# Loading over two queues, softmax inside its PSUM banks, gates and attention weights moved by DMA, and a new order in a one-core transformer block

## The chip, the cores and the metric

The kernel runs on one core of a Trainium2 chip. A core has five instruction streams that work in parallel and meet at semaphores: TensorE (PE in the profile; its weight loads are PEld), VectorE (DVE), ScalarE (ACT), GpSimd (POOL) and SyncE (SP, which here only issues transfers). Transfers are issued by SP or ACT and carried by 16 DMA engines between HBM and the on-chip SBUF. Matmuls write to PSUM, eight banks of 2 KB per partition.

The metric is the device time of one execution in microseconds. The kernel before takes 247.15 us, the median of three runs from 247.07 to 247.26.

## The reference

One sequence of 2048 rows of 512 elements goes through an attention half and a feed-forward half. Both are modulated by a vector `c`.

```python
mod = (silu(c) @ w_mod).reshape(1, 6, 1, -1)
sa, ca, ga, sb, cb, gb = (mod[:, i] for i in range(6))
h = layernorm(x) * (1 + ca) + sa
x = x + ga * A(h, A_wqkv, A_wo)
h = layernorm(x) * (1 + cb) + sb
x = x + gb * B(h, B_w_gate, B_w_up, B_w_down)
```

A is attention with 32 heads of 16 elements. Each row s looks at 8 rows only: s, s-2, ... s-14. `logits = q . k / 4`, with rows before the start masked, a softmax over the 8, and the weighted sum of v, then `@ wo`. B is `(gelu(x @ w_gate) * (x @ w_up)) @ w_down` with 1792 hidden elements. Operands are bf16.

## The kernel before

The 2048 rows are cut into four blocks of 512 rows (`sg` in the code, "block" here), and a block into four chunks of 128 rows (`c4`). Each block goes through the same stages:

- **First norm** (`ln1`): BATCH_NORM_STATS and its aggregate on DVE per chunk (`st`, `mv`), the power -1/2 on POOL (`rstd`), and `xn` on DVE. Block 3's sums are made on ACT instead (`norm_act`).
- **Transpose and modulation** (`transp`, `transp_ev`): `xn` is turned so that features lie on partitions. It is done by PE, 16 matmuls of 128x128 against an identity, for the events in `BY_PE`, and by one DMA transpose on SP for all others; block 0's first norm has its own `transp0`. Then four ACT operations apply scale and shift (`hT` for attention, `h` for the FFN; h0 to h3 in the text).
- **qkv**: twelve groups of four 128x512 matmuls, each moved out of PSUM by an ACT cast into `qT`, `kT` or `vT`.
- **V by DMA** (`vload`): `vT` is stored to DRAM (`vscr`), and four loads bring shifted copies back as `V`, so that the neighbours of a row lie side by side. There is one `V` buffer.
- **Logits**: `pq`, q times eight shifted k, four DVE products of 128x4096 per block; strips of 32 output rows on PE sum them per head into `LTp` (`logits_mm`), which takes two PSUM banks.
- **Softmax** (`soft`): mask for block 0, maximum `mx`, subtraction `z`, exp on ACT, sum `ssum`, reciprocal `rinv`, product `e` (the operation is called p in the text).
- **Turning the weights**: 16 strip matmuls on PE (`PTp`), and two ACT casts into `PT`.
- **Weighted v**: four DVE products `pv` of 128x4096, strips on PE (`o_ps`), ACT casts `oT`, four x_ps groups with `wo`, and `x<-x_ps,x` on DVE, the residual.
- **Second norm** as the first, into `xn2`, then **FFN**: 14 pairs of `g_ps` and `u_ps` groups, gelu (`gl`) and cast (`ub`) on ACT, `hht` = gl x ub on DVE (hh in the text), then `y_ps`, 14 matmuls per chunk, `ot` on DVE and a store per chunk.

Modulation: four of the six parts of `mod` are columns (16 matmuls with one moving column, `cols`, L283); the gates `ga` and `gb` are wanted as rows on all partitions (`gB`), so `row` (L299) multiplies with a broadcast of silu(c), `scB`, in four 128x512 matmuls and an ACT cast. `woscale` and `wdscale` multiply `wo` and `w_down` by the gates on DVE.

**What sets the order.** Each stage is a generator of `Op`s (engine, planned duration, function, events it comes after, buffer slots it takes and gives). `ORDER` at the top of the file, a list of generator numbers, says which generator gives the next operation. The order is thus fixed by hand or by a planner beforehand, and the durations in the `Op`s have no effect on the chip. Each engine executes its own operations strictly in this order, so an instruction that waits holds everything behind it on its engine. This is true of SP's queue of transfers as well: an entry that waits for a semaphore holds the entries behind it.

Slots: `NB` gives buffers per pool, in PSUM `mm` 4 banks, `att` 2, `lg` 2 (one `LTp`). `prod` holds `pq` and `pv`, three buffers.

The head: SP issues x of block 0, chunks 0 and 1, then the `w_mod` parts 1 and 0 (`wm`), then the first third of `wqkv`, x of block 1, and so on (`sp_q`, L259). ACT's queue issues chunk 2, `c` and chunk 3 (`act_q`, L254). PE runs matmuls on zeros (`warmup`) until the first real ones.

In the order of SP's queue before, V of block 0 follows its store directly, then come vT of block 1, `Wg` and `Wu`.

Of the kernel before, what the change touches and what calls it, by code (L numbers as in the profile page):

```python
# [15 lines left out]
NEG = -4.0e9  # L16

ORDER = [
    2, 1, 4, 4, 4, 2, 4, 4, 4, 0, 4, 4, 4, 4, 4, 4, 4, 0, 4, 1, 1, 12, 12, 2, 12, 12, 12, 2, 2, 12, 12, 12, 12,
    12, 3, 3, 12, 12, 4, 4, 4, 4, 3, 3, 13, 3, 3, 3, 11, 13, 14, 2, 2, 2, 2, 2, 2, 2, 4, 4, 14, 14, 4, 4, 2, 11,  # L20
    11, 2, 2, 2, 11, 0, 4, 11, 33, 33, 33, 5, 33, 15, 15, 33, 15, 16, 15, 15, 16, 16, 16, 15, 15, 15, 16, 16,
    16, 18, 75, 15, 15, 15, 16, 15, 33, 75, 75, 33, 33, 33, 33, 16, 16, 16, 16, 34, 34, 75, 75, 35, 6, 2, 2, 2,
    35, 35, 54, 35, 18, 2, 2, 2, 7, 19, 19, 7, 18, 18, 19, 19, 36, 36, 75, 36, 75, 37, 20, 20, 20, 54, 37, 54,
    54, 6, 54, 54, 36, 36, 36, 20, 37, 37, 20, 20, 75, 7, 20, 7, 75, 75, 36, 36, 75, 54, 54, 54, 54, 37, 37, 37,
    20, 20, 20, 10, 36, 75, 75, 75, 75, 55, 55, 38, 2, 2, 37, 56, 56, 56, 56, 36, 36, 36, 37, 37, 21, 21, 37,
    21, 76, 76, 57, 57, 57, 77, 77, 22, 58, 58, 58, 57, 57, 57, 58, 77, 77, 23, 57, 22, 22, 58, 58, 58, 21, 23,
    57, 57, 22, 57, 39, 39, 23, 23, 37, 24, 24, 59, 25, 25, 26, 26, 57, 24, 25, 58, 58, 58, 58, 24, 25, 78, 40,
    78, 26, 26, 26, 78, 79, 2, 79, 79, 39, 39, 26, 78, 78, 78, 78, 26, 26, 26, 26, 79, 79, 79, 79, 78, 40, 27,
    27, 79, 57, 28, 78, 78, 78, 28, 28, 28, 79, 79, 79, 8, 38, 38, 38, 58, 38, 41, 41, 41, 78, 79, 29, 60, 60,
    8, 29, 29, 29, 30, 30, 30, 41, 61, 41, 30, 41, 41, 41, 41, 29, 31, 2, 2, 2, 9, 2, 29, 29, 29, 42, 42, 30,  # L30
    30, 30, 30, 29, 29, 29, 43, 31, 31, 30, 31, 30, 30, 42, 42, 29, 44, 29, 44, 29, 29, 30, 30, 31, 31, 29, 29,
    43, 30, 30, 30, 44, 59, 59, 29, 9, 9, 9, 30, 30, 44, 31, 9, 9, 9, 29, 60, 29, 29, 29, 31, 31, 30, 30, 30,
    45, 45, 46, 29, 59, 30, 29, 47, 46, 29, 47, 30, 30, 45, 45, 31, 31, 46, 46, 29, 29, 29, 31, 30, 30, 30, 30,
    47, 47, 47, 31, 31, 29, 29, 29, 47, 47, 47, 47, 47, 60, 29, 31, 31, 61, 48, 49, 59, 49, 29, 29, 29, 62, 49,
    49, 62, 81, 62, 50, 32, 32, 31, 50, 81, 29, 50, 51, 51, 62, 50, 51, 50, 51, 51, 62, 62, 52, 52, 31, 50, 50,
    51, 51, 62, 62, 62, 52, 82, 32, 50, 63, 63, 51, 50, 50, 51, 51, 50, 50, 51, 50, 51, 52, 52, 52, 64, 50, 63,
    80, 51, 51, 50, 50, 51, 51, 50, 50, 65, 51, 65, 50, 63, 64, 51, 50, 50, 50, 52, 52, 52, 65, 65, 81, 81, 80,
    80, 80, 66, 66, 67, 67, 51, 51, 50, 50, 68, 68, 51, 66, 52, 66, 67, 67, 82, 68, 51, 51, 50, 52, 51, 50, 50,
    50, 51, 68, 68, 68, 32, 83, 51, 51, 51, 50, 52, 52, 52, 50, 50, 50, 50, 50, 68, 68, 80, 68, 83, 83, 68, 69,
    52, 52, 70, 70, 50, 50, 53, 83, 83, 83, 83, 70, 70, 52, 83, 83, 71, 71, 71, 53, 52, 72, 72, 72, 71, 71, 72,  # L40
    71, 71, 71, 53, 84, 84, 73, 72, 72, 72, 72, 85, 71, 71, 71, 73, 73, 72, 86, 86, 71, 72, 72, 71, 71, 73, 71,
    72, 84, 84, 85, 72, 72, 71, 71, 71, 86, 86, 73, 73, 73, 87, 87, 72, 72, 72, 72, 71, 71, 73, 71, 71, 72, 71,
    72, 73, 72, 73, 72, 72, 88, 88, 87, 87, 88, 73, 71, 88, 71, 72, 71, 71, 71, 89, 89, 89, 72, 89, 89, 89, 72,
    72, 72, 73, 71, 73, 73, 89, 89, 89, 89, 71, 71, 71, 71, 71, 90, 91, 91, 91, 91, 53, 73, 73, 71, 71, 92, 74,
    92, 93, 93, 73, 74, 92, 73, 92, 92, 74, 74, 92, 93, 93, 93, 94, 94, 93, 92, 92, 93, 92, 93, 93, 94, 92, 92,
    92, 92, 93, 93, 93, 92, 92, 92, 94, 93, 93, 92, 94, 92, 93, 93, 94, 94, 94, 93, 93, 92, 93, 92, 92, 94, 92,
    93, 94, 93, 93, 92, 92, 92, 94, 93, 93, 93, 92, 92, 92, 93, 93, 93, 92, 94, 94, 94, 92, 92, 92, 92, 92, 94,
    94, 92, 92, 95, 95, 94, 95, 94, 94, 95, 95,
# [52 lines left out]
def kernel(  # L101
# [13 lines left out]
    nc = tc.nc  # L115
# [12 lines left out]
    def pool(name, bufs, **kw):  # L128
# [4 lines left out]
    NB = {"x": 4, "hT": 2, "xn": 2, "q": 4, "vs": 1, "v4": 1, "prod": 3, "lt": 1, "ot4": 1, "h2": 2,  # L133
          "wm": 1, "hh": 16, "o": 2, "wA": 3, "mm": 4, "att": 2, "lg": 1}
    pools = {k: pool(k + "_p", NB[k]) for k in NB if k not in ("mm", "att", "lg", "wm")}
    for k in ("mm", "att", "lg"):
        pools[k] = pool(k + "_p", NB[k], space=PSUM)
    pools["wm"] = pool("wm_p", NB["wm"])
    SL = {k: Slots(NB.get(k, 1)) for k in list(NB) + ["es", "PT"]}
    dram = pool("dram", 1, space=bass.MemoryType.DRAM)  # L140
    vscr = dram.tile([P, 4, VR], BF16, name="vscr")

# [15 lines left out]
    scB = const.tile([P, 4, P], BF16, name="scB")  # L158
# [49 lines left out]
    WM = {1: "h2", 0: "h2", 2: "wm", 3: "h2", 4: "h2", 5: "wm"}  # L208

    def loads():  # L210
# [13 lines left out]
        def ldwm(b, q=nc.sync):  # L224
            def f():
                B["wm", b] = T(WM[b], [P, 4, D], BF16, "wm")
                q.dma_start(
                    out=B["wm", b][:], in_=w_mod[:, b * D:(b + 1) * D].rearrange("(t p) n -> p t n", p=P))
            return f
# [4 lines left out]
        def mb(n):  # L234
            return n / 0.332
# [18 lines left out]
        def act_q():  # L254
            yield Op("ACT", 0.46, ldx(0, 2, 3, nc.scalar), fire="x0.2", lat=0.3, dma=True)
            yield Op("ACT", 0.46, ldc, fire="c", lat=0.0, dma=True)
            yield Op("ACT", 0.46, ldx(0, 3, 4, nc.scalar), fire="x0.3", lat=2.0, dma=True)

        def sp_q():  # L259
            for k in (0, 1):  # L260
                yield Op("SP", 0.47, ldx(0, k, k + 1), fire=f"x0.{k}", lat=0.3)
            yield Op("SP", 0.47, ldwm(1), take=[SL[WM[1]]], fire="wm1", lat=1.0)
            yield Op("SP", 0.5, ldwm(0), take=[SL[WM[0]]], fire="wm0", lat=1.85)
# [6 lines left out]
            yield Op("SP", 0.55, ldwm(2), take=[SL[WM[2]]], fire="wm2", lat=mb(0.5))  # L270
            yield Op("SP", 0.6, ldwm(3), take=[SL[WM[3]]], fire="wm3", lat=mb(0.5))
            yield Op("SP", 0.6, ldwm(4), take=[SL[WM[4]]], fire="wm4", lat=mb(0.5))
            for i in range(4):
                yield Op("SP", 0.45, ld(woP[H * i:H * i + H, :, :], wo_v[i]), fire=f"wo{i}", lat=0.5)
            yield from vload(0)
            yield Op("SP", 0.65, ld(Wg[:], wg_v), fire="Wg", lat=mb(1.75))
            yield Op("SP", 0.65, ld(Wu[:], wu_v), fire="Wu", lat=mb(1.75))
            yield Op("SP", 0.6, ldwm(5), take=[SL[WM[5]]], fire="wm5", lat=mb(0.5))
# [20 lines left out]
    def row(b, dst):  # L299
        def f():  # L300
            ps = T("mm", [P, D], F32, "mb_ps")
            for kt in range(4):
                nc.tensor.matmul(ps[:], lhsT=scB[:, kt, :], rhs=B["wm", b][:, kt, :], start=(kt == 0),
                                 stop=(kt == 3))
            B["mb", b] = ps

        def g():
            nc.scalar.copy(out=dst[:], in_=B["mb", b][:])
        return f, g
# [20 lines left out]
    def mods_ga():  # L330
        f, g = row(2, gB)
        yield Op("PE", 0.9, f, after=["wm2", "scB"], take=[SL["mm"]], give=[SL["wm"]], fire="mb2")
        yield Op("ACT", 0.58, g, after=["mb2"], give=[SL["mm"]], fire="ga")
# [6 lines left out]
    def mods_gb():  # L340
        f, g = row(5, gB)
        yield Op("PE", 0.9, f, after=["wm5", "scB", "woS"], take=[SL["mm"]], give=[SL["wm"]], fire="mb5")
        yield Op("ACT", 0.58, g, after=["mb5"], give=[SL["mm"]], fire="gb")

    def wdscale():
        for h in range(7):
            def wds(h=h):
                w = B["Wd", h // 2][:, 2 * (h % 2):2 * (h % 2) + 2, :]
                nc.vector.tensor_tensor(out=w, in0=w, in1=_ap(gB[:], [[0, 2], [1, D]]), op=ALU.mult)
            yield Op("DVE", 0.63, wds, after=["gb", f"Wd{h // 2}"], fire=f"WdS{h}")  # L350

    def woscale():
        def wos():
            nc.vector.tensor_tensor(out=woP[:], in0=woP[:], in1=_ap(gB[:], [[0, 4], [1, D]]), op=ALU.mult)
        yield Op("DVE", 1.15, wos, after=["ga"] + [f"wo{i}" for i in range(4)], fire="woS")

    def mods2():
        def f1():
            nc.scalar.copy(out=scB[:], in_=_ap(scT[:], [[1, 4], [0, P]]))
        yield Op("ACT", 0.65, f1, after=["scT", "LN1.0.h3.1"], fire="scB")  # L360
# [3 lines left out]
    def norm_act(key, src, ready, ev):  # L364
        k = {}

        for c4 in range(CPS):
# [6 lines left out]
            yield Op("ACT", 0.85, f, after=ready(c4), take=[SL["gl"]], give=[SL["gl"]], fire=f"{ev}.sa{c4}")  # L374
# [3 lines left out]
        yield Op("ACT", 0.2, f, fire=f"{ev}.nm")  # L378

        for c4 in range(CPS):  # L380
# [3 lines left out]
            yield Op("ACT", 0.85, f, take=[SL["gl"]], give=[SL["gl"]], fire=f"{ev}.sq{c4}")  # L384
# [511 lines left out]
```

## Time and profile before

| | us |
|---|---|
| median of three runs | 247.15 |
| the profiled execution | 247.37 |
| its span, first to last instruction | 245.5 |
| first qkv matmul starts | 10.84 |
| first pv of block 0 starts | 41.12 |
| last xn of block 0's second norm ends | 67.25 |
| first FFN matmul starts | 73.83 |
| last `ot` starts | 242.45 |

Times inside the execution count from the start of the span; a timeline row gives start, length and the instruction. The granted clock of TensorE was 1.000 over the span. On PE, a group of four 128x512 matmuls follows the next every 0.86 us. On DVE, the starts of successive instructions of one kind lie closer than the lengths of their rows, because the rows overlap: `pq` and `pv` follow each other every 2.21 us (row 2.28), st with mv every 0.80, an xn every 0.325, the residual every 0.62.

A row of a wait list has who waits, for whom, how long in total, how often, and the longest. A row of a group has line, engine, operation, output and inputs with shapes, count, then busy time and mean ns, then the engine's idle time ahead of it.

### The profile page before, as it was taken

What the parts mean: (1) busy time and instruction counts of PE and PEld (TensorE: products, weight loads), DVE (VectorE), ACT (ScalarE), POOL (GpSimd) and SP (SyncE); (2) the same over time, 40 slices, a digit from 0 to 9 for tenths busy, and PEclk for the clock granted to TensorE, in tenths of its full rate; (3) what the DMA queues carried; (4) which work ended last, traced back from release to release, by engine and by line L of the source; (5) the groups of instructions that cost most, each with busy time, mean ns of one, the idle gap of its engine ahead of it and who ended that gap; (6) DMA issues with size and microseconds to landing.
All of it is one profiled execution on the core that took longest, in us unless ns stands there. A gap on an engine that the chain in (4) does not pass through costs nothing.

```text
span 245.5 us, 3731 instructions
## 1 busy us (share of the span) xinstructions
PE 235.3 (96%) x1431; PEld 110.9 (45%) x1445; DVE 180.0 (73%) x253; ACT 144.0 (59%) x252; POOL 16.6 (7%) x37
## 2 busy tenths in 40 slices
PE   7899678999999999999999999999999999999994
PEld 2655345544453444444444444444444444444444
DVE  4789899989999899898989898677824922222222
ACT  2379698883688576325765835268654424666400
POOL 3450011000400000010000001000000100000000
PEclk9999999999999999999999999999999999999999
DMA  6998699959916009209300592400000061000011
GB/s 168 379 382 269 124 201 250 415 189 217 202 46 208 0 7 211 45 16 201 108 1 3 105 223 44 128 23 0 3 0 0 0 131 64 1 0 3 0 43 43
DMA packets 29289, 27.32 MB, mean 111 GB/s; under 512 B 7256, under 2 KB 28120, under 8 KB 29272
## 3 DMA queue, kind: packets, MB, share of 16 engines
q1 hardware_dynamic: 28976, 26.83, 42.3%
q10 hardware_dynamic: 296, 0.26, 0.4%
q8 instruction: 11, 0.18, 0.3%
q14 instruction: 6, 0.05, 0.1%
HBM read 21.32 MB, written 4.19 MB: 104 GB/s over the span
## 4 chain that ended last, share of the span: by engine, by line
PE 79%; DVE 13%; DMA 4%; POOL 1%; issue 1%; POOLq 0%
PE u_ps L763 19%; PE g_ps L763 19%; PE y_ps L775 18%; PE qkv_ps L556 8%; PE x_ps L735 6%; DMA x<-in_A_x_dram 4%; DVE pq L611 4%; PE o_ps L714 3%; PE LTp L625 2%; DVE st L419 2%; DVE ssum L658 1%; POOL rstd L429 1%; PE y_ps L786 1%; DVE e L669 1%; DVE mx L642 1%; DVE z L648 1%
## 5 line engine op out<-in xcount | busy, mean ns | idle before, releaser
L763 PE MATMUL u_ps<-h,Wu 128*128 128x512 bf16 x224 | 57.5, 379 | 0.0
L763 PE MATMUL g_ps<-h,Wg 128*128 128x512 bf16 x224 | 57.5, 379 | 0.0
L796 ACT ACTIVATE gl<-g_ps 128x512 bf16<-128x512 f32 x56 | 33.6, 601 | 24.9 <-PE g_ps L763 20.6
L775 PE MATMUL y_ps<-Wd,hht 128*128 128x512 bf16 x203 | 45.9, 379 | 0.4
L803 ACT CAST ub<-u_ps 128x512 bf16<-128x512 f32 x56 | 33.0, 589 | 18.2 <-PE u_ps L763 18.1
L814 DVE TENSOR_TENSOR hht<-gl,ub 128x512 bf16<-128x512 bf16 x56 | 22.3, 419 | 29.1 <-ACT ub L803 29.0
L556 PE MATMUL qkv_ps<-hT,wqkv 128*128 128x512 bf16 x184 | 42.2, 380 | 0.0
L700 DVE TENSOR_TENSOR pv<-PT,V 128x4096 bf16<-128x4096 bf16 x16 | 35.8, 2286 | 2.1 <-ACT PT L689 2.1
L611 DVE TENSOR_TENSOR pq<-qT,kT 128x4096 bf16<-128x4096 bf16 x16 | 36.0, 2283 | 0.9 <-PE o_ps L714 0.7
L763 PEld LDWEIGHTS <-Wu 128*128 128x128 bf16 x224 | 21.4, 98 | 27.6 <-issue 2.5
L763 PEld LDWEIGHTS <-Wg 128*128 128x128 bf16 x224 | 21.6, 98 | 26.8 <-issue 1.3
L775 PEld LDWEIGHTS <-hht 128*128 128x128 bf16 x210 | 20.5, 98 | 25.0 <-issue 0.4
L556 PEld LDWEIGHTS <-wqkv 128*128 128x128 bf16 x184 | 20.2, 114 | 19.0 <-issue 2.3
L429 POOL TENSOR_TENSOR rstd<-rstd,neghalf 128x4 f32<-128x4 f32 (+1 forms) x8 | 11.7, 1462 | 174.0 <-DVE rstd L425 174.0
L821 DVE TENSOR_TENSOR ot<-y_ps,x 128x512 bf16<-128x512 f32 x15 | 10.3, 688 | 17.1 <-PE y_ps L775 13.6
L419 DVE BATCH_NORM_STATS2 st<-x 128x6 f32<-128x512 bf16 x28 | 18.9, 675 | 3.0 <-DMA x<-in_A_x_dram 2.9
L489 ACT ACTIVATE h<-h,modT,scl 128x512 bf16<-128x512 bf16 x12 | 8.8, 802 | 15.9 <-DMA h<-xn 15.9
L735 PE MATMUL x_ps<-woP,oT 128*128 128x512 bf16 x60 | 14.9, 379 | 0.2
L570 ACT CAST qT<-qkv_ps 128x512 bf16<-128x512 f32 x16 | 9.5, 601 | 6.5 <-PE qkv_ps L556 5.6
L744 DVE TENSOR_TENSOR x<-x_ps,x 128x512 bf16<-128x512 f32 x16 | 10.7, 684 | 2.7 <-PE x_ps L735 2.7
L572 ACT CAST kT<-qkv_ps 128x512 bf16<-128x512 f32 x16 | 9.5, 602 | 2.8 <-PE qkv_ps L556 2.8
L436 DVE TENSOR_SCALAR xn<-x,mv,rstd 128x512 bf16<-128x512 bf16 x28 | 9.8, 407 | 1.6 <-POOL rstd L429 1.6
(76 smaller groups left out, 175.8 us busy)
## 6 DMA issues: line engine op xcount, KB each, us to landing
V<-vscr SPq DMA_DIRECT2D x12, 520.0 KB, 9.2
wm<-in_w_mod_dram SPq DMA_DIRECT2D x6, 512.0 KB, 7.5
vscr<-vT SPq DMA_DIRECT2D x4, 512.0 KB, 3.8
out_dram<-ot SPq DMA_DIRECT2D x15, 128.0 KB, 1.7
Wg<-in_B_w_gate_dram SPq DMA_DIRECT2D x1, 1792.0 KB
Wu<-in_B_w_up_dram SPq DMA_DIRECT2D x1, 1792.0 KB, 12.8
wqkv<-in_A_wqkv_dram SPq DMA_DIRECT2D x3, 512.0 KB, 8.1
x<-in_A_x_dram SPq DMA_DIRECT2D x3, 512.0 KB, 8.0
```

The costliest lines, as they stand in the source:

```text
L419: nc.vector.bn_stats(out=st_k["st"][:, c4, :], in_=src()[:, c4, :])
L429: nc.gpsimd.tensor_tensor(out=st_k["rstd"][:, a:b], in0=st_k["rstd"][:, a:b], in1=neghalf[:, a:b], op=ALU.pow)
L556: nc.tensor.matmul(ps[:], lhsT=wqkv[blk][:, dt, j::4], rhs=B["hT", sg][:, :, dt, :], start=(dt == 0), stop=(dt == DT - 1))
L611: nc.vector.tensor_tensor(out=pq[:], in0=_ap(B["qT", sg][:, j, :], [[0, W], [1, SG]]), in1=_ap(kT[:, j, sg * SG + 2:sg * SG + 2 + SG], [[2 ...
L700: nc.vector.tensor_tensor(out=t[:], in0=_ap(B["PT", sg][:, 0, :], [[SG, 2], [0, 4], [1, SG]]), in1=_ap(v[:, 0, j, :], [[8, 2], [4 * (SG + ...
L735: nc.tensor.matmul(ps[:], lhsT=B["oT", sg][:, j, c4 * P:(c4 + 1) * P], rhs=woP[:, j, :], start=(j == 0), stop=(j == 3))
L744: nc.vector.tensor_tensor(out=x[:, c4, :], in0=B["x1ps", sg, c4][:], in1=x[:, c4, :], op=ALU.add)
L763: nc.tensor.matmul(ps[:], lhsT=Wt[:, dt, ft * P:(ft + 1) * P], rhs=B["h2T", sg][:, :, dt, :], start=(dt == 0), stop=(dt == DT - 1))
L775: nc.tensor.matmul(ps[:], lhsT=B["hh", sg, ft][:, c4 * P:(c4 + 1) * P], rhs=B["Wd", ft // 4][:, ft % 4, :], start=(ft == 0), stop=(ft == F ...
L796: nc.scalar.activation(out=gl[:], in_=B["g", sg, ft][:], func=ACT.Gelu_apprx_tanh)
L803: nc.scalar.copy(out=ub[:], in_=B["u", sg, ft][:])
L814: nc.vector.tensor_tensor(out=hh[:], in0=B["gl", sg, ft][:], in1=B["ub", sg, ft][:], op=ALU.mult)
```

## The change

- **Head.** All four chunks of x of block 0 and `c` go out on ACT's queue; SP begins with `wm` 1 and 0. The warm-up has 20 matmuls instead of 22.
- **Gates.** `row`, `scB` and the ACT casts go. Parts 2 and 5 of `mod` are made as columns as well; ACT copies them into `gC` as bf16, SP stores these to DRAM (`gscr`, 512 elements, 2 bytes each) and loads them back onto all 128 partitions as `gB`. `w_mod` parts 2 and 5 use the `h2` buffers.
- **Softmax.** `z` is written over the logits in PSUM, and exp, `ssum` and the last product read it there. The SBUF buffer `lt` goes, `LTp` keeps its two banks until the product is done. `prod` has four buffers instead of three, and all strips are handed over per product (`GL`, `GV`).
- **Attention weights of blocks 1 to 3.** No PTp and no casts: the product `e` is stored to DRAM (`escr`, 256 KB), and four loads of 64 KB with runs of 256 bytes bring it back turned, as `PT`.
- **First norms of blocks 2 and 3**: transposed by DMA instead of PE.
- **Order.** A new `ORDER`, and planned durations that have no effect on the chip.

```diff
-    NB = {"x": 4, ..., "prod": 3, "lt": 1, "ot4": 1, "h2": 2, "wm": 1, ...}
+    NB = {"x": 4, ..., "prod": 4, "ot4": 1, "h2": 2, ...}
...
+            yield Op("ACT", 0.46, ldx(0, 0, 1, nc.scalar), fire="x0.0", lat=0.6, dma=True)
+            yield Op("ACT", 0.46, ldx(0, 1, 2, nc.scalar), fire="x0.1", lat=0.5, dma=True)
             yield Op("ACT", 0.46, ldx(0, 2, 3, nc.scalar), fire="x0.2", ...)
             yield Op("ACT", 0.46, ldc, fire="c", lat=0.0, dma=True)
             yield Op("ACT", 0.46, ldx(0, 3, 4, nc.scalar), fire="x0.3", ...)
         def sp_q():
-            for k in (0, 1):
-                yield Op("SP", 0.47, ldx(0, k, k + 1), fire=f"x0.{k}", lat=0.3)
...
+            yield from gload(0)
+            yield Op("SP", 0.6, ldwm(4), take=[SL["h2"]], fire="wm4", lat=mb(0.5))
             yield from vload(0)
...
+    def gload(k):
+        b = (2, 5)[k]
+        def f0():
+            nc.sync.dma_start(out=gscr[b].rearrange("(c p) -> p c", p=P), in_=gC[:, k, :])
+        yield Op("SP", 0.65, f0, after=[f"gc{b}"], fire=f"gst{b}", lat=0.8)
+        def f1():
+            nc.sync.dma_start(out=gB[:], in_=bass.AP(gscr[b].tensor, gscr[b].offset, [[0, P], [1, D]]))
+        yield Op("SP", 0.65, f1, after=[f"gst{b}"] + (["woS"] if k else []), fire=("ga", "gb")[k], lat=0.5)
...
-    BY_PE = ("LN1.1", "LN1.2", "LN1.3", "LN2.0")
+    BY_PE = ("LN1.1", "LN2.0")
...
-    GL = [[1, 1, 1, 1]] + [[2, 2]] * (NSG - 1)
-    GV = [[1, 1, 1, 1]] + [[2, 2]] * (NSG - 1)
+    GL = [[1, 1, 1, 1]] * NSG
+    GV = [[1, 1, 1, 1]] * NSG
...
         def f():
-            B["z", sg] = T("lt", [P, W, P], F32, "z")
+            B["z", sg] = B["LT", sg]
...
+        if sg in PT_DMA:
+            return
...
+    def pt_dma(sg):
+        def f():
+            nc.sync.dma_start(out=escr[sg][:], in_=B["e", sg][:])
+        yield Op("SP", 0.65, f, after=[f"p.{sg}"], give=[SL["es"]], fire=f"est.{sg}", lat=0.7)
+        for a in range(4):
+            def f(a=a):
+                if a == 0:
+                    B["PT", sg] = smp["PT"].tile([P, 2, SG], BF16, name="PT")
+                src = bass.AP(escr[sg].tensor, escr[sg].offset + a * P,
+                              [[W * P, H], [4 * P, 2], [H * W * P, CPS], [1, P]])
+                nc.sync.dma_start(out=B["PT", sg][H * (3 - a):H * (3 - a) + H, :, :].rearrange("p t (g s) -> p t g s", s=P), in_=src)
```

What the new order does around these, read off the two instruction streams:

- DVE, from the first norm of block 1: st of block 1 (the first one ahead of the last two `hT` of block 0), two st of block 2, xn of block 1, the other two st, two pq of block 0, xn of block 2, two pq, woP, mask, mx, z, xn of block 3, pq, ssum, rinv, p, pq, four pv, two pq of block 1, residual and second norm of block 0 with mx and z of block 1 between its statistics and its xn, then ssum, rinv, p of block 1, three pq of block 2, two hh, pq, four hh, four pv of block 1.
- PE: after the first five qkv groups of block 0 come the columns of gate `ga` and the transposes of block 1, then the v groups. Groups of block 2 and 3 are taken forward; behind the transposes of block 0's second norm three qkv groups are left ahead of the first FFN matmul, where there were five and the gate row.
- SP: wm 1, wm 0, wqkv, x 1, wqkv, wqkv, x 2, x 3, wm 2, wm 3, wo, gate store, gate load, wm 4, vT store 0, transpose of block 2, three V loads of block 0, vT store 1, the fourth V load, transpose of block 3, Wg, vT store 2, Wu, wm 5, V of block 1, weights of block 1 (store, three loads), gate store, the fourth load, gate load, w_down, vT store 3, V of block 2, and so on.

## The prediction

> **What bounds the kernel now.** I read the page's busy shares and slices first, then PE's list of waits, then the chain of waits in order of time, then busy time by stretch, then the DVE groups by shape and the DMA issues. A block is 512 rows, numbered 0 to 3. "Group" means four 128x512 matmuls into one PSUM bank (0.86 us in the chain). Four-strip matmuls (LTp, o_ps, PTp) are called strips.
>
> ```profile
> PE 235.3 (96%) x1431; PEld 110.9 (45%) x1445; DVE 180.0 (73%) x253; ACT 144.0 (59%) x252; POOL 16.6 (7%) x37
> PE   7899678999999999999999999999999999999994
> DVE  4789899989999899898989898677824922222222
> DMA  6998699959916009209300592400000061000011
> ```
> PE is full from the seventh slice on; DVE is full until two thirds of the span; the DMA engines are full in the first tenth.
>
> ```profile
> PE LTp L625 <- DVE pq L611: 2.1, 2, 1.6
> PE PTp L680 <- DVE e L669: 1.8, 2, 1.4
> PE modT_ps L289 <- ACT vT L576: 0.5, 1, 0.5
> ```
> After its start PE waits for almost nothing but DVE's attention products and softmax.
>
> ```profile
> 33.32 1.85 DVE ssum L658
> 35.20 0.96 DVE rinv L664
> 36.18 1.24 DVE e L669
> 37.46 0.62 PE PTp L680 x16
> 38.08 0.98 PE qkv_ps L556 x4
> 39.07 0.89 PE hTp L451 x16
> ...
> 125.15 0.55 PE PTp L680 x16
> ```
> The chain runs over DVE until block 0's softmax, then over PE. It prices the pieces that move: 0.89 us for a block's 16 transposes, 0.55 for 16 PTp matmuls, and 0.98 instead of 0.86 for the group behind a strip.
>
> ```profile
> 12.20:73.83 61.63, 57.41 (x419) 29.98 (x420) 57.46 (x71) 47.87 (x92) 8.28 (x4) 1.00 0.86 229
> 73.83:242.45 168.62, 167.62 (x933) 75.25 (x941) 114.52 (x162) 92.08 (x152) 3.10 (x3) 1.00 0.25 58
> ```
> Columns: length, then busy PE, PEld, DVE, ACT, POOL. 73.83 is the first FFN matmul. Leg 2, behind it, is PE with 1.0 us idle; leg 1, ahead of it, has DVE and PE equally full.
>
> ```profile
> L658 DVE TENSOR_REDUCE ssum<-z 128x128 f32<-128x1024 f32 x4 | 7.6, 1910 | 0.0
> L642 DVE TENSOR_REDUCE mx<-LTp 128x128 f32<-128x1024 f32 x4 | 4.9, 1222 | 0.9 <-PE LTp L625 0.9
> L648 DVE TENSOR_TENSOR z<-LTp,mx 128x1024 f32<-128x1024 f32 x4 | 4.9, 1222 | 0.1
> ```
> ```profile
> V<-vscr SPq DMA_DIRECT2D x12, 520.0 KB, 9.2
> out_dram<-ot SPq DMA_DIRECT2D x15, 128.0 KB, 1.7
> h<-xn SPq DMA_TRANSPOSE x3, 4.2
> ```
> The same reduction takes 1222 ns from PSUM and 1910 from SBUF; transfers take 1.7 us (a store) to 9.2 (a V load) to land.
>
> **Leg 2, worked on PE.** Removed: PTp of blocks 1 to 3, 3 x 0.55 = 1.65. The strips stand in 8 runs instead of 11 (all of a block's LTp in one run, the PTp runs gone): 3 x (0.97 - 0.86) = 0.33. The one wait before PTp of block 1, 0.44, goes with it. 168.62 - 2.42 = 166.2.
> What stands behind the removed PTp: p -> a 256-KB store -> four 64-KB loads -> pv, where it was p -> 0.55 PE -> 1.07 ACT. No row shows these transfers. Store: vscr<-vT, twice as large, takes 3.3 to 3.9 (SP queues its next entries behind that wait). Loads: four issues of 0.62 (plus one gate store among them in block 1), the last landing 1.7 later; their 256-byte packets, 16 per DMA engine and load, cost between 18.7 ns (the DMA transpose: 2080 packets under 512 B in 2.4 us, 130 per engine) and 81 ns (a V load: 1-KB packets, 520 KB in 2.6 us), so 1.2 to 5.2 us for all four, of which 3.1 lies under the issues. Together 7.6 to 10.9 us; I take 8.6, nearer the transposes, whose packets have this size. Cover on DVE between p and pv: block 1 four pq x 2.21 + six hh x 0.335 = 10.85; block 2 two ot x 0.62 + three pq + three hh = 8.9; block 3 three ot, each behind 3.0 us of y_ps on PE, and two hh, over 9. So 0 to 2.0 us late in block 2 alone; I take 0.4. Without the cover the price were the whole 7 us a block, since hh, and then PE's PSUM banks, queue behind pv. Leg 2: 166.6.
>
> The Trainium skill, page "DMA: Bandwidth & Descriptors", section "Why small descriptors are slow (HBM only)", gives a 256-byte descriptor 27% overhead; by that our loads cost about 0.9 us each instead of 0.7, an estimate inside the bounds above. The transposes' rate here (277 GB/s inside one) agrees that SBUF to SBUF shows no such penalty.
>
> **Leg 1, worked on DVE**, which sets it. The load stream starts with wm1 at 0.80 instead of 1.71 on SP, while x of block 0 goes out on ACT's queue. x of block 1 keeps its place in the stream, so lands 0 to 0.9 earlier than 11.5; but h2.1 and h3.1 (0.65) now stand behind its first st. DVE is through these at 12.1 to 13.0; I take 12.4 (before: 12.38 for the same work). Head: no gain.
> From there to the last xn of block 0's second norm, at the spacing of the trace: eleven st+mv x 0.80 = 8.8 and four rstd inputs 0.6; four sets of xn x 1.3 = 5.2; woP 1.13; mask 0.3; softmax 0 with ssum at the PSUM price 1.26+1.14+1.26+0.98+1.14 = 5.8; twelve pq/pv x 2.21 = 26.5; four x x 0.62 = 2.5; and now mx, z of block 1, 2.4: 53.2. Before, the same list (ssum 1.94, no mx, z) gives 51.5, with 2.6 of waits 54.1, and 54.87 was measured: I add the missing 0.7. Waits now: the four rstd powers (1.05) lie under st, pq or mx+z; LTp of block 0 under woP; ssum waits 0.3 for exp (table load 1.28 + 1.06 against one pq); pv of block 0 waits for V.
> V of block 0: mp2 and the transposes of block 1 (done when xn is, 17.9, + 0.9) now stand before the v groups on PE: + four groups, and h x 4 and four casts on ACT, so vT is complete at 24.2 instead of 21.6. The store lands 3.9 later, 28.2. Three V loads land 10.5 later at 38.7, the fourth, now behind vT of block 1, at 41.3 to 44.6 (2.6 per 512 KB). DVE wants it at 43.1 by the same list. 0 to 1.5, I take 0.6.
> SP's queue ahead of it: the gate store waits for its ACT copy (18.4), the gate load for the store, then wm4, then vT. The store has 512 packets of 2 bytes, 32 per engine, behind loads that end at about 20; at 18.7 to 81 ns it lands by 22.0 to 24.0, and vT is free to go at 23.3 to 25.3: hidden, or 1.1 late.
> xn ready at 12.4 + 53.2 + 0.7 + 0.9 = 67.2 (before 67.25: DVE gains only mx, z). Behind it PE has 0.1 + transposes 0.89 + three qkv groups 2.6; before it had the transposes, five groups, the gate row (0.87) and a strip, 6.6 in all. First FFN matmul at 70.8 instead of 73.83. PE can do this: its work from the first qkv (10.84) is 48 groups 41.5, two transposes 1.8, four mod columns 1.9, strips 7.0, x_ps 3.5: 56, so done by 67 even with no wait moved, and 4 us of its waits are free. The 32 transposes and the gate row that leave PE (1.8 + 0.8) are therefore worth only what the reordering makes of them. The DMA transposes land 4.2 after xn in block 2 (needed 10 later) and, behind V, at 44 to 46.5 in block 3, where qkv wants h at 49; 1 us late is in the 4 us.
>
> [...] If ssum in PSUM took 1910 all the same, leg 1 would be 0.65 longer and the sum 243.1.
>
> **Sum.** 70.8 + 166.6 = 237.4 for the last ot; behind it 3.05 as before: span 240.5; plus the 1.87 that the profiled run (247.37) has around its span: 242.4. That is 5.0 under the profiled run, 4.75 under the median, 247.15; the profiled run stands 0.22 above the median, so the same sum on it reads 242.2. I forecast 242.4. Own range 241.4 to 243.6.
>
> **Rivals.** A difference under 0.2% (0.5 us) can't be told from none.
> (a) Slower: the gate stores of 2 bytes. Their price stands in no row. For each us past 22.95 that the first lands, vT, V and all pv of block 0 come a us later; the second stands before the last PT load of block 1, where 0.5 to 2 us are free. To give 5 us back, 32 packets must take about 5.5 us, 170 ns each, twice the dearest row. At 200 ns: 4.9 + 3.4 late, 250.7. For it: SP waits for the landing with vT queued behind. Against: both rows. The Trainium skill's DMA page, section "Specifications", has transfers under 512 B do a read-modify-write; no run here shows its price.
> (b) Smaller gain: every round trip at its upper bound. V 1.5 instead of 0.6, PT of block 2 late by 2.0 instead of 0.4, ssum at 1.94: +0.9 +1.6 +0.65 = 245.6; 244 to 246.2.
> (c) No change: the order puts PE's waits elsewhere in leg 1 (as the DVE sum is the same, 67.2 against 67.25, a PE wait of 3 us behind it is enough), and 2 more in leg 2: 247.
> (d) Larger gain: no wait for V, PT or exp, and the head 0.4 earlier: 240.7.
>
> **Chances.** Forecast 0.46, (a) 0.17, (b) 0.23, (c) 0.04, (d) 0.10. Faster 0.79, same 0.04, slower 0.17. Range 240.8 to 247.2: it takes in (b) and leaves out (a) and most of (d).
>
> **What would show it.** PE's wait lists: none for PTp past block 0; PE idle under 1 us behind the first FFN matmul, which starts at 70 to 72. ssum at 1.2 to 1.3 us. A gate store to landing under 4 us. pv of block 0 starting at 43 to 44.6, released by DMA V or PT. DVE idle before pv of block 2 under 2 us. I am wrong if DVE's pv waits several us for a DMA, if x of block 0 lands later than 6.5 behind wm1, or if PE waits in leg 2.

## The result and the profile after

The changed kernel is slower: 270.23 us (median of four runs, 269.04 to 271.86) against 247.14. The ratio is 1.0938, 95% interval 1.0877 to 1.0999. The profiled execution takes 271.86, its span is 269.8. First the page of the changed kernel: busy times, then the 40 slices (6.7 us each) of PE, DVE, the granted clock and the DMA engines.

```profile
PE 238.4 (88%) x1387; PEld 110.2 (41%) x1387; DVE 176.7 (65%) x253; ACT 139.2 (52%) x245; POOL 14.4 (5%) x37
PE   7699830499999999178999999999999999999995
DVE  3799704668999980299999998775584772222222
PEclk9689995589999999759999999999999999999999
DMA  6991007999999210397942105926200004100011
```

PE and DVE have two holes: DVE at slices 6 and 16, PE at 6 to 8 and 17. Ahead of each the DMA row is almost empty too (4 to 6, then 14 to 16): for a while hardly anything runs, transfers included. The clock falls to 5 tenths in or behind a hole. By stretch (length, then busy PE, PEld, DVE, ACT, POOL, clock, DMA share, GB/s), leg 1 from 13.6 us on and leg 2 from the first FFN matmul to the last `ot`:

```profile
13.60:89.49 75.89, 60.32 (x430) 30.48 (x429) 56.96 (x75) 46.73 (x92) 6.78 (x8) 0.88 0.76 186
89.49:266.94 177.45, 168.86 (x895) 74.94 (x893) 112.09 (x160) 88.95 (x146) 3.10 (x3) 0.97 0.31 68
```

The first FFN matmul starts at 89.49 (before 73.83, predicted 70.8), and leg 2 takes 177.45 (before 168.62, predicted 166.6). Both legs are missed: by 18.7 and by 10.9. Two rows of PE's waits and one of ACT's between them, then two rows of DVE's:

```profile
PE qkv_ps L551 <- ACT vT L571: 14.9, 3, 11.7
ACT vT L571 <- DMA vscr<-vT: 14.0, 1, 14.0
PE o_ps L727 <- DVE pv L713: 7.6, 3, 6.2
```
```profile
DVE woP L354 <- DMA gB<-gscr: 12.5, 1, 12.5
DVE pv L713 <- DMA PT<-escr: 11.6, 1, 11.6
```

Each engine names the next, and in the end a DMA. What these DMAs wait for stands in SP's queue (start, length of the issue, what was issued):

```profile
22.75 0.39 SPq L306 DMA_DIRECT2D gscr<-gC  x1
38.79 0.34 SPq L310 DMA_DIRECT2D gB<-gscr  x1
...
39.71 0.63 SPq L577 DMA_DIRECT2D vscr<-vT  x1
...
47.28 1.97 SPq L586 DMA_DIRECT2D V<-vscr  x3
...
94.58 0.55 SPq L306 DMA_DIRECT2D gscr<-gC  x1
95.17 0.56 SPq L700 DMA_DIRECT2D PT<-escr  x1
110.15 0.34 SPq L310 DMA_DIRECT2D gB<-gscr  x1
```

The store of a gate, 1 KB, holds SP for 16.0 us until the load that needs it may go, and vT of block 0 with it: its last cast ended at 27.95, its store goes out at 39.71. The second time the last PT load of block 1 stands directly behind the store: SP issues it at once, but in the chain of waits it lands 17.12 us later, and pv of block 1 starts at 112.70.

### The profile page after: what moved, and what is told of

It reads as the page before. It is cut to its first block, busy times and chain, and to the rows that moved or that the text cites. A ratio compares the mean times of both kernels' runs of the same rounds, so it can differ in the third digit from the quotient of the medians.

```text
span 269.8 us, 3646 instructions
## 1 busy us (share of the span) xinstructions
PE 238.4 (88%) x1387; PEld 110.2 (41%) x1387; DVE 176.7 (65%) x253; ACT 139.2 (52%) x245; POOL 14.4 (5%) x37
## 4 chain that ended last, share of the span: by engine, by line
PE 70%; DMA 18%; DVE 5%; ACT 3%; issue 2%; ACTq 1%; SPq 1%; DVEq 0%
PE y_ps L788 17%; PE g_ps L776 15%; PE u_ps L776 15%; PE qkv_ps L551 11%; DMA PT<-escr 6%; DMA gscr<-gC 6%; PE x_ps L748 5%; DMA hT<-xn 4%; DMA x<-in_A_x_dram 2%; PE o_ps L727 2%; DVE pv L713 2%; DVE Wd L349 2%; PE LTp L620 1%; PE y_ps L799 1%; PE warm_ps L207 1%
## 5 line engine op out<-in xcount | busy, mean ns | idle before, releaser
L551 PE MATMUL qkv_ps<-hT,wqkv 128*128 128x512 bf16 x184 | 45.0, 396 | 15.6 <-ACT vT L571 14.9
L776 PE MATMUL g_ps<-h,Wg 128*128 128x512 bf16 x224 | 58.4, 384 | 0.0
L776 PE MATMUL u_ps<-h,Wu 128*128 128x512 bf16 x224 | 58.1, 382 | 0.0
L713 DVE TENSOR_TENSOR pv<-PT,V 128x4096 bf16<-128x4096 bf16 x16 | 35.9, 2286 | 12.9 <-DMA PT<-escr 11.6
L827 DVE TENSOR_TENSOR hht<-gl,ub 128x512 bf16<-128x512 bf16 x56 | 22.3, 420 | 26.3 <-ACT ub L816 26.3
L424 POOL TENSOR_TENSOR rstd<-rstd,neghalf 128x4 f32<-128x4 f32 (+1 forms) x8 | 9.6, 1202 | 182.4 <-DVE rstd L420 182.4
L571 ACT CAST vT<-qkv_ps 128x512 bf16<-128x512 f32 x16 | 8.7, 607 | 18.4 <-DMA vscr<-vT 14.0
L738 ACT CAST oT<-o_ps 128x512 bf16<-128x512 f32 x16 | 9.1, 591 | 17.3 <-PE o_ps L727 17.3
L727 PE MATMUL o_ps<-pv,Msum 128*32 128x512 bf16 x128 | 9.6, 411 | 7.6 <-DVE pv L713 7.6
## 6 DMA issues: line engine op xcount, KB each, us to landing
V<-vscr SPq DMA_DIRECT2D x12, 520.0 KB, 10.4
Wu<-in_B_w_up_dram SPq DMA_DIRECT2D x1, 1792.0 KB, 10.4
```

The source lines that it names most:

```text
L551: nc.tensor.matmul(ps[:], lhsT=wqkv[blk][:, dt, j::4], rhs=B["hT", sg][:, :, dt, :], start=(dt == 0), stop=(dt == DT - 1))
L713: nc.vector.tensor_tensor(out=t[:], in0=_ap(B["PT", sg][:, 0, :], [[SG, 2], [0, 4], [1, SG]]), in1=_ap(v[:, 0, j, :], [[8, 2], [4 * (SG + ...
L727: nc.tensor.matmul(o_ps[H * i:H * i + H, :], lhsT=M2[:], rhs=B["pv", sg, j][:, t, i, :], start=(t == 0), stop=(t == 1), tile_position=(0, ...
L776: nc.tensor.matmul(ps[:], lhsT=Wt[:, dt, ft * P:(ft + 1) * P], rhs=B["h2T", sg][:, :, dt, :], start=(dt == 0), stop=(dt == DT - 1))
L827: nc.vector.tensor_tensor(out=hh[:], in0=B["gl", sg, ft][:], in1=B["ub", sg, ft][:], op=ALU.mult)
```

## The experiments

Theory 1: the gate stores of 2-byte elements hold SP's queue, twice. Theory 2: x of block 0 and `c` on ACT's queue start the kernel late, and the rest follows. Theory 3: the new order and the round trips cost this much anyway.

**gate_row** mends the stores alone. PE makes the gate as one row, with 4 matmuls of a one-column weight in place of 16 with one moving column, so that it lies on one partition.

```diff
-    gC = const.tile([P, 2, 4], BF16, name="gC")
+    gR = const.tile([1, D], BF16, name="gR")
-            nc.sync.dma_start(out=gscr[b].rearrange("(c p) -> p c", p=P), in_=gC[:, k, :])
+            nc.sync.dma_start(out=gscr[b].rearrange("(o n) -> o n", o=1), in_=gR[:])
-        yield Op("PE", 0.43, cols(b), ...)
+                nc.tensor.matmul(ps[0:1, :], lhsT=scT[:, kt:kt + 1], rhs=B["wm", b][:, kt, :], ...)
```

> The gate goes to DRAM as one row of 1 KB from one partition (PE makes it with a one-column weight, 4 x 0.22 us) instead of 512 packets of 2 bytes; nothing else differs from the changed kernel. Theory 1 (the 2-byte stores hold SP's queue): the store lands in about 2 us instead of 15.6, the woP wait of 12.5 and the pv wait of 11.6 go, 246 to 250 us. Theory 2 (the late start and the lowered clock carry through): 264 to 268. Theory 3 (V, PT and the transposes by DMA are too slow of themselves): the waits of vT and pv stay above 5 us each, 255 to 263.

243.97 us (243.77 to 244.98), ratio to before 0.9853 [0.9793, 0.9913]. SP's queue in it:

```profile
22.94 0.28 SPq L306 DMA_DIRECT2D gscr<-gR  x1
24.17 0.36 SPq L310 DMA_DIRECT2D gB<-gscr  x1
```

The same 1 KB, from one partition in one packet, holds SP for 1.2 us. The first FFN matmul starts at 74.20, leg 2 takes 166.03, and neither woP nor pv of block 1 waits for a DMA. That is 26.3 us for one access pattern; Theory 3 falls for all but a small rest of leg 1.

**old_head** puts x chunks 0 and 1 of block 0 back to SP ahead of `wm`; **row_head** is both edits.

```diff
-            yield Op("ACT", 0.46, ldx(0, 0, 1, nc.scalar), ...)
-            yield Op("ACT", 0.46, ldx(0, 1, 2, nc.scalar), ...)
+            yield Op("ACT", 0.46, ldx(0, 0, 1, nc.sync), ...)
+            yield Op("ACT", 0.46, ldx(0, 1, 2, nc.sync), ...)
```

> Chunks 0 and 1 of x of block 0 go out on SP ahead of wm, as before; the rest is the changed kernel. First qkv matmul at about 11 instead of 14.9. Theory 1: the gate store still lands 15.6 after a copy that comes 4 us earlier, 265.5 to 267.5 us. Theory 2: the clock stays at 1.0 through the first 30 us and more than the 4 us comes back, under 262.

> Both edits at once. Theory 1: what is left of the change is what the prediction summed, 242 to 246 us, PE idle behind the first FFN matmul under 2 us. Theory 3: above 250, with DVE's pv waiting for V or PT.

old_head 264.83 (264.07 to 267.03), 1.0713 [1.0639, 1.0788]: 5.4 below the changed kernel, a little more than Theory 1 allowed (265.5) and less than Theory 2 asked for (262). Both long waits stay (woP 8.7 us, pv 10.4). row_head 244.06 (243.26 to 244.44), 0.9855 [0.9802, 0.9909], the same as gate_row. Theory 2 falls as the main cause. The old head starts qkv at 12.19 instead of 14.43, and the first FFN matmul at 73.17 instead of 74.20, but the time doesn't tell the two apart. Nor does one trace price a head: with the same old head, qkv started anywhere from 10.86 (pt_pe, below) to 14.06 us (v_ltp).

**gate_8b** keeps the columns and orders them so that a partition's four elements lie side by side: 128 packets of 8 bytes.

```diff
-                    nc.tensor.matmul(ps[:, ch:ch + 1], lhsT=B["wm", b][:, kt, ch * P:(ch + 1) * P],
+                    nc.tensor.matmul(ps[:, ch:ch + 1], lhsT=B["wm", b][:, kt, ch::4],
-            ... out=gscr[b].rearrange("(c p) -> p c", p=P)
+            ... out=gscr[b].rearrange("(p c) -> p c", c=4)
```

> The gate's columns are taken interleaved, so the same 1 KB goes to DRAM in 128 packets of 8 bytes instead of 512 of 2. If each small packet costs its own time to land (13.7 us over 512), the store lands in about 5.3 us and the kernel takes 248 to 253 us. If any packet far under 512 bytes is equally slow as a whole transfer, 15 us and 269 to 271. If only writes under 4 bytes are slow, 2 us, and the time of the kernel with the row.

247.94 (245.89 to 249.19), 1.0004 [0.996, 1.0048].

```profile
22.32 0.35 SPq L306 DMA_DIRECT2D gscr<-gC  x1
25.49 0.34 SPq L310 DMA_DIRECT2D gB<-gscr  x1
```

3.2 us, between 1.2 and 16.0, and the gain is gone, but not by the length of the stores alone. The first FFN matmul is at 77.70, 3.5 later than in gate_row; leg 2 is the same (166.02), though the second store takes 4.0. In leg 1 vT of block 0 goes out no later than in gate_row (27.56 against 28.25). What comes later is the DMA transpose of block 2 behind it: ACT starts on its result at 36.93 instead of 34.63, and PE waits 3.0 us. From 40 to 50 us the granted clock is then 0.72 (1.00 in gate_row). Why this transpose lands later isn't shown.

**first_row** mends only the first of the two stores.

> The changed kernel with only the first gate made as a row and stored in one packet of 1 KB; the second gate is still stored as 512 elements of 2 bytes. If each store holds SP's queue for itself (Theory 1), the first costs what lies in leg 1 and the second only what lies behind the first FFN matmul: the first FFN matmul at 74.2 as in gate_row, DVE's pv of block 1 waits 10 to 12 us for DMA PT, the last ot some 11 later than in gate_row (240.2), time 253 to 256. If the second store only hurts because everything was already late, its wait is under 3 us and the time 244 to 247.

252.57 (249.8 to 253.36), 1.0199 [1.0127, 1.0271]: 8.6 above gate_row, so the rest of the 26.3, 17.7, belongs to the first store. The first FFN matmul is at 74.73, as expected. SP's queue and pv of block 1:

```profile
78.93 0.55 SPq L310 DMA_DIRECT2D gscr<-gC  x1
79.52 0.56 SPq L713 DMA_DIRECT2D PT<-escr  x1
92.76 0.34 SPq L314 DMA_DIRECT2D gB<-gscr  x1
```
```profile
93.32 2.29 DVE L726 TENSOR_TENSOR pv<-PT,V 128x4096 bf16<-128x4096 bf16 x1 [6.76 <-DMA PT<-escr]
```

The wait is 6.8, not the expected 10 to 12. In the changed kernel it was 11.6: there the store took 15.6 and not 13.8, the load landed 2.1 and not 0.1 us behind it, and DVE wanted pv 1.1 sooner after the store's issue. The wait stands on its own, not as a follow-on of the first: leg 2 is 172.8, 6.8 longer than in gate_row.

**v_first, ltp_first, v_ltp** ask for the 2.4 us by which the first FFN matmul of row_head (73.17) misses the forecast. DVE's rows of row_head:

```profile
DVE LTp L638 <- PE LTp L626: 1.9, 1, 1.9
...
DVE pv L719 <- DMA V<-vscr: 0.8, 1, 0.8
```

Only the place of an operation in the hand-written order changes: v_first issues the fourth V load of block 0 ahead of the store of vT 1; ltp_first puts the last two LTp strips ahead of the qkv group that waits for a PSUM bank; v_ltp does both.

> row_head (gates as rows, the old head) with SP's fourth V load of block 0 issued directly behind the third, ahead of the store of vT of block 1. If V is what pv of block 0 waits for in row_head (0.83 us behind DMA V), pv of block 0 starts at 45.7 to 46.0 instead of 46.60 and the first FFN matmul at 72.3 instead of 73.17: time about 243.2. If the LTp strip of block 0 decides (DVE idle 1.95 ahead of the mask), the start of pv moves by no more than 0.8 and the wait ahead of the mask stays 1.9.

> row_head with PE's last two LTp strips of block 0 moved ahead of the qkv group that waits 0.70 us for a PSUM bank behind ACT's four squares. DVE's wait ahead of the mask should fall from 1.95 to about 0.3. If V comes no earlier, the gain is lost again at pv of block 0, whose wait for DMA V grows from 0.83 to about 2.4: first FFN matmul within 0.2 of 73.17, time 244.0. If V's wait was only a follow-on of DVE's, the first FFN matmul comes 1.6 earlier, time 242.4.

> row_head with both moves. If the two waits of leg 1 stand in series behind one another as the traces say, both moves together give what neither gives alone: pv of block 0 at 44.2 to 45, first FFN matmul at 70.9 to 71.6, leg 2 166.0 as before, time 241.9 to 242.6. If PE is the limit of leg 1, the first FFN matmul stays at 72.5 or later and the time at 243.5 or more.

v_first 245.65 (0.9929 [0.9898, 0.9961]), ltp_first 243.25 (0.9858 [0.9817, 0.9898]), v_ltp 246.13 (0.9957 [0.9925, 0.999]). The first move loses, and both together lose as well (row_head: 244.06): my expectation of 241.9 to 242.6 was wrong. ACT in v_first:

```profile
48.01 0.58 ACT L589 CAST vT<-qkv_ps 128x512 bf16<-128x512 f32 x1 [2.70 <-PE qkv_ps L569]
```

The row names PE, but PE ran the PTp that stands behind this group at 45.48, so the group was done. This cast writes vT of block 2 into the one vT buffer, and must wait until the store of vT 1 has read it; that store now stands behind the fourth V load. The casts of PT are queued behind this cast, and pv waits 2.8 us for them. (That it is the store is inferred from the order and the single buffer; no row names it.) ltp_first did what was expected at the mask, but the wait moved on:

```profile
DVE ssum L671 <- ACT LTp L666: 2.0, 2, 1.8
DVE pv L731 <- DMA V<-vscr: 0.8, 1, 0.8
```

exp stands on ACT behind three `hT` operations and four casts, so `ssum` gets the 1.8 us that the mask no longer waits. Its time can't be told from row_head's. Leg 1 has several waits in parallel there (PSUM banks, ACT's order, V), and taking one away uncovers the next.

**act_store** is old_head with the same 2-byte stores issued on ACT's queue. The first gate load and the scaling of `woP` stand later in the order, so that nothing of SP's is queued behind the stores.

```diff
-            nc.sync.dma_start(out=gscr[b].rearrange("(c p) -> p c", p=P), in_=gC[:, k, :])
+            nc.scalar.dma_start(out=gscr[b].rearrange("(c p) -> p c", p=P), in_=gC[:, k, :])
+MOVE = [('ga', 'LN1.3.t'), ('woS', 'pv.0.0')]
```

> old_head, with both gate stores still 512 elements of 2 bytes, but issued on ACT's queue; the first gate load is issued on SP behind the fourth V load of block 0 instead of ahead of wm 4, and woP is scaled directly ahead of pv of block 0. Nothing of SP's stands behind the first store any more, and no PT load behind the second. If what a store of 2-byte elements holds is its own queue (Theory 1), SP's transfers land as in row_head while it is under way, pv of block 0 starts at 46 to 48 and the time is 243.5 to 246, although each store still takes 13 to 16 us to land. If it holds the DMA engines, which all queues share, V of block 0 and the last PT load of block 1 come as late as in old_head: first FFN matmul past 80 and 255 to 265.

263.51 (262.12 to 265.37), 1.0625 [1.0528, 1.0721], about the time of old_head (264.83): the own queue is not what is held, and Theory 1 falls in that part. SP's queue in two places, and the packets from 88 to 92 us:

```profile
27.42 12.30 SPq L464 DMA_TRANSPOSE hT<-xn  x1
...
82.95 0.36 SPq L704 DMA_DIRECT2D escr<-e  x1
98.20 2.54 SPq L712 DMA_DIRECT2D PT<-escr  x4
```
```profile
DMA packets 0, 0.00 MB, mean 0 GB/s; under 512 B 0, under 2 KB 0, under 8 KB 0
```

ACT issued the stores at 22.70 and 82.40. The 256-KB store of the weights, issued by SP 0.5 us after the second, lands only 15.2 us later (2.0 in row_head), though no engine moves a packet from 88 to 92. The 528 packets of ACT's queue had all run by 84, but this store lands 15.4 us after its issue, at 97.8, just ahead of the 256-KB store at 98.2. So here the small writes had left the DMA engines quickly, and what was issued behind them on the other queue was not reported as landed before they were. A transpose within SBUF, issued on SP 4.7 us after the first store, was slow as well (16.1 us to landing; the median of row_head's two is 6.0). Which part of the memory path holds them isn't shown.

**gate_pe** undoes the gates' move: rows on PE with the broadcast `scB`, ACT casts to `gB`, on the old head. **pt_pe** turns the weights of blocks 1 to 3 on PE again, all else as in row_head.

```diff
+                nc.tensor.matmul(ps[:], lhsT=scB[:, kt, :], rhs=B["wm", b][:, kt, :], ...)
+            nc.scalar.copy(out=gB[:], in_=B["mp", b][:])
-            nc.sync.dma_start(out=gscr[b]..., in_=gC[:, k, :])
-            nc.sync.dma_start(out=gB[:], in_=bass.AP(gscr[b].tensor, ...))
```
```diff
-            nc.sync.dma_start(out=escr[sg][:], in_=B["e", sg][:])
+                        nc.tensor.matmul(PTp[H * (3 - a):H * (3 - a) + H, :, q:q + P], ...)
-                nc.sync.dma_start(out=B["PT", sg][H * (3 - a):H * (3 - a) + H, :, :]..., in_=src)
+                    nc.scalar.copy(out=B["PT", sg][:, :, a * 256:a * 256 + 256], in_=B["PTp", sg, a][:])
```

> The gates undone alone, on the old head: both gate rows are made on all partitions by PE with a broadcast silu(c) (four 128x512 matmuls) and cast to gB by ACT, as before the change; the gate stores and loads go, all else as in row_head. If moving the gates by DMA is worth only PE's 2 x 0.4 us and ACT's casts, which the waits of leg 1 hide, the time is that of row_head, 243.6 to 244.8, first FFN matmul 72.8 to 73.6. If SP's waits for the gate in row_head (1.2 us) still cost, it is below 243.4.

> row_head with the attention weights of blocks 1 to 3 turned on PE and cast by ACT as before the change; escr and its transfers go, the rest of the order is kept (PTp directly ahead of the second, tenth and third g_ps group). The prediction took 1.65 us of PTp and up to 0.33 of strip runs off PE for the DMA way, so leg 2 should be 1.6 to 2.4 us longer than in row_head (166.02): 167.6 to 168.4, the time 245.6 to 246.5. If PE had that time to spare in leg 2, leg 2 stays within 0.5 of 166.02 and the time at 244.

gate_pe 243.56 (242.54 to 243.59), 0.9803 [0.9717, 0.9889]: no worse than the mended DMA way, so the gates' move is worth nothing even when its stores are quick. pt_pe 247.13 (246.0 to 248.07), 0.9986 [0.9945, 1.0027], 3.1 above row_head: without the weights' move, in this placement of PTp and its casts, the gain is gone. Leg 2 by stretch, pt_pe first (74.00 to 243.00, where its leg is 73.81 to 242.99), then row_head:

```profile
74.00:243.00 169.00, 167.94 (x942) 75.27 (x940) 111.93 (x161) 91.05 (x152) 3.10 (x3) 1.00 0.26 61
```
```profile
73.17:239.19 166.02, 165.62 (x888) 74.56 (x893) 112.06 (x160) 88.78 (x146) 3.10 (x3) 1.00 0.30 73
```

PE has 2.3 us more work, and 0.7 more idle time (one wait of 1.0 for ACT, which the PT casts of block 1 hold; I placed them there). Leg 2 is 3.2 longer, beyond the expected 1.6 to 2.4 by about that wait; so some 2 us of it are the move's own worth.

**probe** prices the stores by themselves in a quiet stretch.

```diff
+        nc.sync.dma_start(out=to(32, 32), in_=of(32))      # step, elements of a piece
+        nc.sync.dma_start(out=to(512, 1), in_=of(1))
+        nc.sync.dma_start(out=to(32, 1), in_=of(1))
+        nc.sync.dma_start(out=to(1, 1), in_=of(1))
+        nc.sync.dma_start(out=prb[0:1, :], in_=gB[0:1, :])
+        nc.sync.dma_start(out=prb[0:1, :], in_=gB[0:1, :])
```

> gate_pe with six extra stores to a scratch tensor in DRAM, issued on SP behind the last output store of block 1 (about 161 us), where SP has nothing to issue for 30 us; each waits for the one before it, so the distances of their issues are the times to landing. In order: 512 pieces of 64 bytes, close together; 512 of 2 bytes, 1 KB apart; 512 of 2 bytes, 64 bytes apart; 512 of 2 bytes side by side, as in the change; one of 1 KB; one of 1 KB. The outputs are those of gate_pe. If a piece costs because it is a packet, whatever its size and place, all four stores of 512 take 13 to 16 us. If it costs because it is smaller than some unit that must be read and written back, the 64-byte store is quick (under 5) and the three of 2 bytes take 13 to 16. If it costs because many writes fall into the same unit one after another, only the store side by side takes 13 to 16 and the other three are under 5. The 1-KB store takes 1.2 as in gate_row. Where the sum passes 30 us, the transpose of block 2's second norm is late and the time longer by that.

One run, 242.44. SP's queue:

```profile
160.63 0.46 SPq L868 DMA_DIRECT2D prb<-gB  x1
164.51 0.37 SPq L869 DMA_DIRECT2D prb<-gB  x1
166.86 0.36 SPq L870 DMA_DIRECT2D prb<-gB  x1
168.62 0.36 SPq L871 DMA_DIRECT2D prb<-gB  x1
182.84 0.30 SPq L872 DMA_DIRECT2D prb<-gB  x1
183.96 0.23 SPq L873 DMA_DIRECT2D prb<-gB  x1
```

The distances of the starts: 512 pieces of 64 bytes 3.9 us (behind two output stores in the queue); 512 of 2 bytes, 1 KB apart, 2.4; 64 bytes apart, 1.8; side by side, 14.2; one of 1 KB, 1.1. Number and size of the packets are the same in the second to the fourth: only the distance of the addresses differs. Of the three readings only the third fits: writes of a few bytes that fall next to one another are what costs. On average that is (14.2 - 1.1) / 512 = 26 ns a piece; the 8-byte pieces of gate_8b come to (3.2 - 1.2) / 128 = 16 ns. That they are served strictly one after another, and how large the unit is within which they disturb each other, isn't shown; at a distance of 64 bytes they no longer do.

## Why the prediction was wrong

**The step that failed** is the price of the gate store: "512 packets of 2 bytes, 32 per engine ... at 18.7 to 81 ns it lands by 22.0 to 24.0 ...: hidden, or 1.1 late." That is 0.6 to 2.6 us for the packets. In the changed kernel the store took 15.9 us from issue to landing, 0.5 us for each of an engine's 32, six times my upper bound. The two rows I bounded it by were of larger pieces, and they measure the engines' time; that was right (the packets had run 2 us after the issue). The landing is what SP waits for, and it is another quantity. By the probe it hangs on the addresses: the same 512 pieces land in 1.8 us when they lie 64 bytes apart. The unknown had no upper bound in the trace, and I gave it one.

**Rival (a)** named the place and the wait, vT queued behind a store that SP waits for, with too small a price: 200 ns a packet, 4.9 + 3.4 late and 250.7. That price was one for an engine's packets, which isn't what was dear. Measured by first_row against gate_row the second store costs 8.6 in time, and by the changed kernel against first_row (270.23 - 252.57) the first 17.7. The Trainium skill's page "DMA: Bandwidth & Descriptors", section "Specifications", which (a) named, has a read-modify-write for transfers under 512 bytes and says nothing there of where they fall. By the probe the size alone doesn't decide: 2-byte pieces 64 bytes apart took 1.8 us, side by side 14.2.

**The second store** I had down with "0.5 to 2 us are free" ahead of the last PT load of block 1. The load was held 17.1 us. That queue place, not PT's own round trip, made DVE wait.

**Leg 2 otherwise** came out as worked: 166.03 in gate_row (forecast 166.6, with 0.4 for a late PT of block 2 that didn't occur: no pv waited for PT there). The weights' round trip was taken at 8.6 within 7.6 to 10.9; in gate_row p of block 1 ends at 74.06 and the last load is issued at 79.10, which with the median 2.4 to landing gives 7.4. Even the lower bound was a little dear.

**Leg 1 otherwise** was too short by 3.4: the first FFN matmul of gate_row is at 74.20, not 70.8. All of it is there when pv of block 0 starts, at 47.29 instead of 43.7 (43.1 and 0.6 for V); from there on it took 26.9, forecast 27.1. Two terms add up to it. "Head: no gain", with DVE through block 0's `hT` at 12.4: it is through at 13.96 there, since with four chunks and `c` in one queue the last `st` starts at 8.33 (before 6.54). And "LTp of block 0 under woP": DVE waits 1.95 for it, because PE runs into its four full PSUM banks, which ACT empties only after four squares of block 3's norm (this is inferred; the row of PE's wait, 0.69, names ACT's copy into `modT` behind them). 1.56 + 1.95 = 3.5. This is a sum of one trace's rows, not shown by a run that takes a term away: row_head and ltp_first gained 1.0 and 0.7 at the first FFN matmul, and no time beyond the spread. Nor is a difference of 1 us there safe: gate_pe and probe, alike up to that point, start it at 72.24 and 71.33. The gate's copy and vT of block 0 were forecast too early as well (18.4 and 24.2; in gate_row they end at 22.9 and 28.2).

**ssum from PSUM** was right:

```profile
L637 DVE TENSOR_REDUCE mx<-LTp 128x128 f32<-128x1024 f32 x4 | 4.9, 1220 | 0.0
L653 DVE TENSOR_REDUCE ssum<-LTp 128x128 f32<-128x1024 f32 x4 | 4.9, 1219 | 4.6 <-ACT LTp L648 4.6
```

1219 ns, forecast 1.2 to 1.3; from SBUF it was 1910. The other case that the forecast priced, 1910 from PSUM as well, didn't occur.

**Of the signs named beforehand**, pv waiting several us for a DMA, x of block 0 late (the fourth `st` starts at 8.85, 8.05 behind `wm` 1's issue) and PE waiting in leg 2 all came true.

With the stores mended the sum would have been 1.2 to 1.7 us below the measured 243.56 (gate_pe) to 244.06 (row_head), at the upper end of the forecast's own range of 241.4 to 243.6 or just above it; the forecast's sign was that of all other parts together. In that, leg 1 was 3.4 too short and leg 2 0.6 too long (gate_row).

## What to carry to other kernels

Price a DMA that others wait for by its landing, and look at where its pieces fall in memory: 1 KB written as 512 neighbouring 2-byte pieces took 14 to 16 us, as one row 1.1 to 1.2. Before a transfer is put into a queue, look at what is issued behind it, in other queues as well; here two stores of 1 KB, one ahead of vT's store and one ahead of a PT load, cost 26 us together. Where several waits end close together, as in leg 1 here, moving one operation forward mostly hands the time to the next wait.

## What the runs showed of the hardware beyond that

- The DMA engines looked idle while small writes were under way: no packet from 88 to 92 us in act_store, a share of 0.01 from 26 to 38 us in the changed kernel. An empty DMA row doesn't mean that no transfer is outstanding.
- Such stores delay later transfers of another queue: a 256-KB store 15.2 us instead of 2.0.
- A hole in PE's work went along with a lower granted clock. In the changed kernel it was 0.50 from 40 to 50 us, while PE was busy for 1.87 of these 10 us, and still 0.69 from 50 to 60, with PE busy for 7.27. In gate_8b PE's one wait of 3.0 us, up to 39.67, was followed by 0.72 from 40 to 50, with PE busy throughout.
